# The first three groups of a fused attention and feed-forward kernel: squares moved to ScalarE, factors loaded and multiplied in another way, and another order of calls

## The chip, the cores and the metric

One core of one Trainium2 chip. The time is that of one execution on the device, in microseconds (us), the median of several runs. The engines are named as the profile names them: PE (TensorE), PEld (its weight loads), ACT (ScalarE), DVE (VectorE), POOL (GpSimd) and SP (SyncE, which here only issues DMAs). POOL issues DMAs too, on a queue of its own; that queue takes the loads in which float32 becomes float16.

## The reference

```python
def rmsnorm(x, g):
    rms = np.sqrt(np.mean(x * x, axis=-1, keepdims=True) + 1e-06)
    return x / rms * g
q_n, k_n = rmsnorm(q, g_q), rmsnorm(k, g_k)        # q, k, v: (8, 12, 448, 64)
scores = 1.0 / np.sqrt(64) * np.matmul(q_n, k_n.transpose(0, 1, 3, 2))
scores = scores - np.max(scores, axis=-1, keepdims=True)
attn = np.exp(scores)
attn = attn / (np.sum(attn, axis=-1, keepdims=True) + 1e-09)
attn_out = np.matmul(attn, v)
x = attn_out.transpose(0, 2, 1, 3).reshape(3584, 768)
h = x @ w_in                                       # w_in: (768, 2048)
g = np.maximum(h, 0.0) + alpha * np.minimum(h, 0.0)
out = g @ w_out                                    # w_out: (2048, 768)
```

## The kernel before

There are eight batches of twelve heads. The kernel works in 24 groups `y`, three per batch, each of four heads (two and two, in the two halves of the partitions). A group goes through these steps, each a function that the plan calls:

- `load_qk(y)`: SP loads q and then k of the group, 448 KB each, into buffers. Groups 0, 1, 3 and 4 use four buffers that are lent on in turn; groups 2, 5 and 8 use a part of one large tile, `arena`. A load waits until the last reader of what its buffer held before has finished, and SP issues its loads strictly in order.
- `square(y, q or k)`: x times x; for the first nine groups this is on POOL, with the exception of `square(1,q)`, which is on ACT. `reduce` sums over the 64 elements of a head on DVE, `root` makes x to the power of -0.5 of the mean with two ACT instructions (a logarithm and an exponential), and `scale` multiplies, on DVE for the groups 0 to 3 and on POOL after that. `qs` is the result, in float16.
- `turn(y)`: seven transposes of q and seven of k on PE, and two DVE copies that put them into `qT` and `kT`. The copy of k multiplies by `gain`, the product of g_q and g_k for each of the 64 elements. `turn_one` does it for q or k alone. From group 9 on DVE's own transpose takes its place (`flip`, and `weigh` for the gain).
- `score(y,j)` and `soft(y,j)`, for the seven key tiles j: four matmuls (eight later) into PSUM, then the exponential on ACT.
- `den`, `log`, `invert`: sums over the keys by matmuls with ones, and their reciprocal by a logarithm and an exponential on ACT. `attend` multiplies by v on PE, `times` multiplies by the reciprocal on DVE and writes `xT`. `den(0+1)` and what follows it takes two groups at once, `den(2)` the third one of the batch.

For each batch `b` then follow `up(b,ft)`, for 16 tiles ft of the hidden layer (six matmuls with `w_in_sb`), `slope` (times alpha, mostly on ACT) and `larger` (the maximum, on DVE), which write `gT`; and `down` and `down_end`, the second product and its copy, or from tile 6 on products of sums and differences of blocks (`mix_two`, `qa1` and the like; `mix_weights` prepares them on POOL). For batch 0 `begin(ft)` does four of the six matmuls of the first four tiles before group 2's `xT` is there.

Group 0 is done in pieces by functions of its own: `part_square`, `part_reduce`, `part_root`, `part_scale`, `part_turn`, `part_copy`. `opening()` issues the loads of groups 0 to 2 on SP and those of alpha, g_q and g_k on POOL, and has PE transpose alpha and the g's (tile `ct`), from which `gains()` makes `cols` and `gain` on DVE. `spin(n)` runs matmuls whose result nobody reads.

`load_w_in(c)`, `load_w_out(c)` and `load_v(b)` are issued by POOL. A chunk c of w_in is four loads of 128 KB (as written) for the rows up to 512, and with c even four more for the rest. The completion of POOL's DMAs is counted on eight semaphores in turn, so POOL waits, before it issues a load, until the eighth load before that one has landed.

The order of all this is written out by hand: `PLAN` is a text with 1,325 calls that are made one after the other. Each engine executes its own instructions in the order of the calls; only semaphores stand between engines. A call of the plan moved ahead of another therefore changes the order on each engine that both use, and on no other.

`follow(y, nm)` is a POOL copy of one element that reads `qs`, so that POOL waits at that point for whoever wrote it.

## Time and profile before

| | |
|---|---|
| median of 3 runs | 411.84 us (411.53 to 413.08) |
| the profiled execution | 410.69 us |
| its span, from the first to the last instruction | 408.6 us |
| granted TensorE clock, mean | 1.000 |
| busy: PE, DVE, ACT, POOL | 395.3, 268.3, 270.4, 299.9 us |
| DMA | 58.39 MB moved, 143 GB/s in the mean |

The profile is of one execution. Busy times are shares of the span; a matmul's row includes the time until its result is out, so consecutive rows overlap, and times from row to row are differences of starts. `hT` are the products of `up`, `sc` the scores, `tps` and `tps2` the transposes, `nat` and `arena` the loaded q and k with their squares, `rr` the roots. Queue q1 of the DMA rows is SP's, q0 is POOL's. Lines such as L376 are those of the kernel before.

### The profile page before, as it was taken

To read this page: it belongs to the slowest core of one execution; us is meant where nothing else is said; L and a number is where in the kernel's file an instruction comes from. 1 tells how busy PE (TensorE), PEld (TensorE's weight loads), DVE (VectorE), ACT (ScalarE), POOL (GpSimd) and SP (SyncE) were. 2 spreads that over 40 slices of the span, in tenths; PEclk is the share of its full clock that TensorE was granted. 3 is DMA by queue.
4 is the path that set the end of the run, shared out by engine and by line. 5 is a ranking of instruction groups with operands and counts; after the bars stand their busy time and mean duration, and the time that the engine had idled before them with its cause. 6 is when DMAs were issued, how large, how long until landed. Compare 5 with 4: busy or idle time off the path is not lost.

```text
span 408.6 us, 11992 instructions
## 1 busy us (share of the span) xinstructions
PE 395.3 (97%) x5083; PEld 210.3 (51%) x5083; DVE 268.3 (66%) x480; ACT 270.4 (66%) x405; POOL 299.9 (73%) x200
## 2 busy tenths in 40 slices
PE   7688999999999999999999999999999999999996
PEld 3344445555455445554455455555555455655664
DVE  3957874676766685779678678886668545654422
ACT  5597686757885876767886987686876874245110
POOL 7977998497796998997796995589496809600780
PEclk9999999999999999999999999999999999999999
DMA  7999699796776794579952595794516000230143
GB/s 260 242 280 227 110 265 165 173 239 177 125 180 154 173 203 108 119 172 185 232 130 83 136 240 145 147 217 102 140 38 131 21 2 22 59 79 0 39 98 98
DMA packets 37222, 58.39 MB, mean 143 GB/s; under 512 B 4769, under 2 KB 28977, under 8 KB 37169
## 3 DMA queue, kind: packets, MB, share of 16 engines
q1 hardware_dynamic: 23232, 45.43, 43.2%
q0 software_dynamic: 13536, 11.81, 19.1%
q8 instruction: 39, 0.64, 0.7%
q10 hardware_dynamic: 400, 0.39, 0.3%
q14 instruction: 15, 0.11, 0.1%
HBM read 58.40 MB, written 11.01 MB: 170 GB/s over the span
## 4 chain that ended last, share of the span: by engine, by line
PE 88%; DVE 4%; DMA 3%; POOL 3%; issue 1%; POOLq 0%; DVEq 0%
PE hT L726 25%; PE hTa L726 9%; PE sc L588 8%; PE op L792 7%; PE qx L854 5%; PE av L613 5%; PE qz L854 4%; PE qc L854 4%; PE oq L854 4%; PE qxa L854 3%; PE avb L613 2%; PE dn L613 2%; PE oqm L854 2%; DMA w_in_sb<-in_moe_w_in_dram 2%; POOL nat L376 2%; DMA arena<-in_g_k_dram 2%
## 5 line engine op out<-in xcount | busy, mean ns | idle before, releaser
L602 ACT ACTIVATE expT<-sc 128x896 f16<-128x896 f32 x168 | 146.3, 916 | 40.9 <-PE sc L588 39.2
L726 PE MATMUL hT<-xT,w_in_sb 128*128 128x448 f16 x558 | 115.9, 353 | 1.6 <-DVE xT L709 1.4
L726 PEld LDWEIGHTS <-w_in_sb 128*128 128x128 f16 x768 | 73.0, 98 | 74.5 <-issue 9.9
L423 POOL TENSOR_TENSOR qs<-nat,rr 128x896 f16<-128x896 f32 x30 | 65.7, 2221 | 26.5 <-ACT rr L417 23.4
L766 ACT ACTIVATE gT<-hT,cols 128x448 f16<-128x448 f32 x92 | 58.4, 636 | 40.0 <-PE hT L726 38.9
L772 DVE TENSOR_TENSOR gT<-hT,gT 128x448 f16<-128x448 f32 x93 | 57.3, 619 | 38.2 <-ACT gT L766 37.5
L365 POOL TENSOR_TENSOR nat<-nat 128x896 f32<-128x896 f32 x30 | 50.7, 1697 | 8.1 <-DMA nat<-in_q_dram 7.7
L588 PE MATMUL sc<-qT,kT 64*32 64x448 f16 (+1 forms) x1092 | 49.4, 355 | 4.3 <-ACT expT L602 1.7
L854 PEld LDWEIGHTS <-gT 128*128 128x128 f16 x352 | 33.4, 98 | 25.5 <-issue 4.1
L726 PE MATMUL hTa<-xT,w_in_sb 128*128 128x448 f16 x198 | 42.9, 353 | 0.0
L842 POOL TENSOR_TENSOR gs<-gT 128x1024 f16<-128x1024 f16 x4 | 8.5, 2127 | 36.7 <-DVE gT L772 36.7
L709 DVE TENSOR_TENSOR xT<-av,rden 64x448 f16<-64x448 f32 (+1 forms) x37 | 27.2, 736 | 10.7 <-ACT rden L671 4.6
L386 DVE TENSOR_REDUCE sp<-nat 128x28 f32<-128x896 f32 x30 | 32.1, 1070 | 2.1 <-POOL nat L365 2.0
L588 PEld LDWEIGHTS <-kT 64*32 64x32 f16 (+1 forms) x1092 | 16.7, 93 | 32.4 <-issue 23.0
L792 PE MATMUL op<-w_out_sb,gT 128*128 128x384 f16 x176 | 30.3, 326 | 0.2 <-DVE xT L709 0.2
L766 ACT ACTIVATE gT<-hTa,cols 128x448 f16<-128x448 f32 x33 | 21.0, 636 | 10.5 <-PE hTa L726 10.0
L772 DVE TENSOR_TENSOR gT<-hTa,gT 128x448 f16<-128x448 f32 x33 | 20.4, 618 | 10.6 <-ACT gT L766 10.2
L613 PEld LDWEIGHTS <-vt 64*32 64x32 f16 x1344 | 19.7, 92 | 12.2 <-issue 1.9
L792 PEld LDWEIGHTS <-gT 128*128 128x128 f16 x192 | 18.3, 98 | 14.5 <-issue 3.0
L613 PE MATMUL av<-expT,vt 64*32 64x448 f16 x896 | 24.3, 350 | 0.0
L850 POOL TENSOR_TENSOR gT<-gT 128x1024 f16<-128x1024 f16 x11 | 23.5, 2133 | 0.0
L854 PEld LDWEIGHTS <-arena 128*128 128x128 f16 x136 | 12.6, 98 | 10.5 <-issue 2.3
(151 smaller groups left out, 572.5 us busy)
## 6 DMA issues: line engine op xcount, KB each, us to landing
nat<-in_q_dram SPq DMA_DIRECT2D x60, 216.0 KB, 4.1
nat<-in_k_dram SPq DMA_DIRECT2D x60, 216.0 KB, 5.0
out_dram<-osb SPq DMA_DIRECT2D x107, 96.0 KB, 3.1
vt<-in_v_dram POOLq DMA_DIRECT2D x8, 672.0 KB, 7.8
w_in_sb<-in_moe_w_in_dram POOLq DMA_DIRECT2D x24, 128.0 KB, 7.3
w_out_sb<-in_moe_w_out_dram POOLq DMA_DIRECT2D x4, 768.0 KB, 8.6
nat<-in_k_dram SPq DMA_DIRECT2D x6, 448.0 KB, 7.8
nat<-in_q_dram SPq DMA_DIRECT2D x5, 448.0 KB, 6.7
```

What stands on the lines that cost most here:

```text
L365: nc.gpsimd.tensor_mul(out=sqs[y, nm], in0=t[:, :, :HD], in1=t[:, :, :HD])
L386: nc.vector.tensor_reduce(out=parts[y][:, ts("qk".index(nm), 4 * J), :1], in_=sqs[y, nm], axis=AXIS_X, op=ALU.add,)
L423: nc.gpsimd.tensor_mul(out=t.rearrange("p j d n -> p n j d"), in0=nat[y, nm][:, :, :HD].rearrange("p (n j) d -> p n j d", j=J), in1=r.unsq ...
L588: nc.tensor.matmul(out=sc[ds(64 * g + m * c, m), par, :S].rearrange("p (j c) -> p j c", j=J), lhsT=kT[ds(64 * par, 64), j, g, ts(c, m)], r ...
L602: nc.scalar.activation(out=expT[y][:, j], in_=scs[y, j][:, :, :S], func=AF.Exp, scale=QK_SCALE, bias=EXP_BIAS,)
L613: nc.tensor.matmul(out=accs[g][ds(32 * n, 32), :S], lhsT=weights(g, y, par, c, j), rhs=expT[y][ds(64 * g, 64), j, par, :], start=(j == 0), ...
L709: nc.vector.tensor_mul(out=o, in0=p, in1=q)
L726: nc.tensor.matmul(out=hT[:, :S], lhsT=w_in_sb[:, block_of(g, i), ts(ft, 128)], rhs=xT[b][:, g, i, :], start=(i == 0 and g == 0), stop=(i ...
L766: nc.scalar.activation(out=g, in_=hT[:, :S], func=AF.Copy, scale=alpha_sb[:, ft : ft + 1])
L772: nc.vector.tensor_max(out=g, in0=hT[:, :S], in1=g)
L792: nc.tensor.matmul(out=op[:, :OH], lhsT=gT[:, ft, ts(tile % J, 128)], rhs=w_out_sb[:, ft, ts(oh, OH)], start=(ft == 0), stop=(ft == NF - 1),)
L854: nc.tensor.matmul(out=bank[:, c], lhsT=g[:, ft], rhs=v[:, ft, c], start=(first and ft == 0), stop=(ft == HF - 1), skip_group_check=True,)
```

## The change

Four functions take another form, and the plan is another one up to the scores of group 8, the last of batch 2 (the third batch); from there on it is the same text. In the functions:

- `square` takes the engine and the number of pieces from the plan. Both squares of group 1 are on ACT now, q and k; before, k's was on POOL. `square(2,q)` is one instruction instead of two.
- `opening` loads g_q and g_k with one DMA each, written twice side by side, instead of two, and ahead of alpha. It no longer spins and no longer transposes; `factors()` does that, as a call of the plan, into a score buffer.
- `gains` makes `gain` by a tensor_scalar that reads one factor from PSUM and the other as its scalar.
- `load_w_in(c, lo, hi)` issues a part of the loads of a chunk. `slope` takes its engine from the plan, and `part_copy` could use ACT for k, which the plan doesn't do.

In the plan, the roots of group 0's k are one call, `part_root(k,0:7)`, ahead of group 1's squares, where there were two calls behind `square(1,q)`; k's scales of group 0 stand ahead of `gains()`, and `reduce(1,q)` behind it; the first `spin` calls are others (17 narrow ones first instead of two wide and 17 narrow ones). Further on, `load_qk(3)`, `load_qk(4)` and `load_qk(6)` are called later or earlier than before among calls of other engines, with the same order on SP. w_in's chunk 2 is loaded with its second half first. `times(2,0,0)` stands ahead of `reduce(4,k)`; before, it stood behind it. `soft(2,0)` stands ahead of `soft(1,4)` and `den(0+1,0)`. `scale(7,q)` stands behind `scale(7,k)` and `mix_weights(0,2)`. The calls before and after, up to group 1's first scores:

```diff
-opening() part_square(q,0:1,0:7,act) part_square(q,1:2,0:7,act) part_reduce(q,0:1,0:7) spin(2,0)
-part_reduce(q,1:2,0:7) part_root(q,0:7) part_square(k,0:2,0:3,act) part_scale(q,0:7,7,pool)
-part_reduce(k,0:2,0:3) part_square(k,0:2,3:7,act) square(1,q) load_w_in(1) spin(1)
-part_reduce(k,0:2,3:7) part_root(k,3:7) reduce(1,q) square(1,k) part_root(k,0:3) gains()
-part_turn(q,r0-7) load_qk(3) spin(1,0) part_scale(k,0:3,3,vec) part_turn(k,r0-3)
-part_scale(k,3:7,4,vec) part_copy(q,0:7,vec) part_turn(k,r3-7) load_v(0) reduce(1,k) follow(0,k)
-square(2,q) part_copy(k,0:3,vec) part_copy(k,3:7,vec) root(1) square(2,k) score(0,0,0) soft(0,0)
+opening() part_square(q,0:1,0:7,act) part_square(q,1:2,0:7,act) part_reduce(q,0:1,0:7) spin(17,0)
+part_reduce(q,1:2,0:7) spin(1,0) part_root(q,0:7) part_square(k,0:2,0:3,act)
+part_square(k,0:2,3:7,act) part_scale(q,0:7,7,pool) part_reduce(k,0:2,0:3) part_reduce(k,0:2,3:7)
+spin(2) load_w_in(1,0,4) part_root(k,0:7) part_turn(q,r0-7) part_copy(q,0:7,vec) load_v(0)
+square(1,q,act) spin(3,0) square(1,k,act) factors() spin(3,0) part_scale(k,3:7,4,vec)
+part_scale(k,0:3,3,vec) part_turn(k,r0-3) square(2,q) spin(1,0) square(2,k) gains() reduce(1,q)
+part_turn(k,r3-7) part_copy(k,0:3,vec) part_copy(k,3:7,vec) reduce(1,k) spin(1,0) score(0,0,0)
+score(0,4,1) spin(1,0) load_w_in(0,0,4) soft(0,0) load_w_in(0,4,8) reduce(2,q,1) root(1) spin(1)
```

Around the calls of which the prediction speaks further on:

```diff
-score(2,5,0) square(4,k) load_qk(6) reduce(4,q,None) soft(2,3) soft(2,2) soft(2,5) den(2,0) log(2)
-reduce(4,k,None) invert(2) attend(2,0,1) score(3,0,1) square(5,q) square(5,k) times(2,0,0)
...
-soft(3,2) larger(0,5) up(0,6,0) scale(4,k) turn(4) scale(5,q) up(0,8,0) score(4,0,0) slope(0,6)
+soft(2,5) den(2,0) log(2) square(5,q) invert(2) square(5,k) reduce(4,q,None) attend(2,0,1)
+times(2,0,0) reduce(4,k,None) score(3,1,0) reduce(5,q) square(6,q) reduce(5,k) score(3,0,1) begin(1)
...
+larger(0,2) slope(0,5) larger(0,3) soft(3,2) up(0,6,0) larger(0,5) scale(4,k) load_qk(7) turn(4)
+scale(5,q) up(0,8,0) slope(0,6) soft(3,6) score(4,0,0) square(6,k) scale(5,k) score(3,5,0)
```

The functions:

```diff
-        if (y, nm) == (1, "q"):
-            nc.scalar.activation(out=sqf, in_=src, func=AF.Square)
-        else:
-            n = 2 if (y, nm) in ((2, "q"), (G, "k")) else 1
-            for h in range(n):
-                c = ts(h, 2 * J * D // n)
+        for h in range(n):
+            c = ts(h, 2 * J * D // n)
+            if eng is nc.scalar:
+                nc.scalar.activation(out=sqf[:, c], in_=src[:, c], func=AF.Square)
+            else:
                 nc.gpsimd.tensor_mul(out=sqf[:, c], in0=src[:, c], in1=src[:, c])
...
     def opening():
         load_qk(0)
         nc.scalar.preload_act_table_set("natural_log_exp_and_others")
+        for n, g in enumerate((g_q, g_k)):
+            nc.gpsimd.dma_start(
+                out=rows[NF + n : NF + n + 1].rearrange("o (h d) -> o h d", h=2),
+                in_=g.unsqueeze(0).unsqueeze(0).broadcast_to((1, 2, D)),
+            )
         nc.gpsimd.dma_start(out=rows[:NF], in_=moe_alpha.rearrange("(t p) -> t p", p=128))
-        for n, g in enumerate((g_q, g_k)):
-            for h in range(2):
-                nc.gpsimd.dma_start(
-                    out=rows[NF + n : NF + n + 1, ds(64 * h, 64)], in_=g.unsqueeze(0)
-                )
         load_qk(1, True)
         load_qk(2)
 
-        spin(2)
-        spin(17, False)
-        ct = psf.tile([128, 512], FP32, name="ct", tag="mm")
+    def factors():
+        ct = pss.tile([128, 2, 512], FP32, name="ct", tag="sc")[:, 0]
         nc.tensor.transpose(ct[:, : NF + 2], rows, ident32[: NF + 2, : NF + 2])
         held_ct.append(ct)
 
     def gains():
         nc.vector.tensor_copy(out=cols, in_=held_ct[0][:, : NF + 2])
-        nc.vector.tensor_mul(
-            out=gain, in0=cols[:, NF : NF + 1], in1=cols[:, NF + 1 : NF + 2]
+        nc.vector.tensor_scalar(
+            out=gain, in0=held_ct[0][:, NF : NF + 1], scalar1=cols[:, NF + 1 : NF + 2],
+            scalar2=None, op0=ALU.mult,
         )
```

More of the change, by code (lines that the diff above doesn't have):

```diff
@@ new lines @@
+larger(1,13) larger(1,14) soft(8,3) score(8,5,1) log(6+7) larger(1,15) flip(9,k) weigh(9)
+score(8,1,0) down(3,0,0) scale(10,q) square(11,k) down_end(2,1) score(8,2,0) scale(10,k) flip(9,q)
+soft(8,5) reduce(11,k) reduce(11,q) soft(8,4) soft(8,1) score(8,6,0) fold(11) load_qk(13)
+attend(6+7,0,0) attend(6+7,1,0) score(9,1,0) score(9,0,0) down_end(3,0) soft(8,2) invert(6+7)
+score(9,2,1) down(3,1,0) times(6+7,0,0) soft(8,6) root(11) times(6+7,1,0) load_qk(14) flip(10,q)
+down(4,0,1) mix_weights(1,2) soft(9,0) times(6+7,1,1) score(9,5,0) square(12,q) soft(9,1) soft(9,2)
@@ L358, in load_w_out, with square @@
         )
-    def square(y, nm):
+    def square(y, nm, eng=None, n=1):
         if y >= TD:
@@ L493, in part_copy @@
         tp = tops["ps", nm][:, j]
-        if nm == "k":
+        if nm == "k" and eng is nc.scalar:
+            nc.scalar.activation(out=o, in_=tp, func=AF.Copy, scale=gain[:, 0:1])
+        elif nm == "k":
             nc.vector.tensor_scalar(
```

198 lines of the change are left out of this document (96 added, 102 removed).

## The prediction

> **What bounds the kernel now.** I read the page first, then the busy time by stages, then TensorE's instructions in order of time, and from the places where it stood idle I went back through the other engines' instructions to what they waited for.
>
> ```profile
> span 408.6 us, 11992 instructions
> PE 395.3 (97%) x5083; PEld 210.3 (51%) x5083; DVE 268.3 (66%) x480; ACT 270.4 (66%) x405; POOL 299.9 (73%) x200
> ```
>
> ```profile
> 20.00:30.00 10.00, 8.51 (x157) 4.38 (x160) 5.57 (x9) 9.70 (x15) 7.69 (x12) 1.00 1.12 282
> 30.00:40.00 10.00, 9.57 (x242) 4.85 (x226) 7.19 (x9) 7.75 (x9) 7.31 (x10) 1.00 1.14 240
> 40.00:50.00 10.00, 8.77 (x62) 4.65 (x61) 8.60 (x14) 6.10 (x12) 9.98 (x8) 1.00 0.56 82
> 50.00:60.00 10.00, 9.82 (x80) 4.60 (x78) 7.29 (x11) 8.94 (x13) 9.97 (x8) 1.00 1.16 279
> ```
>
> The columns after the stretch's length are busy us of PE, PEld, DVE, ACT, POOL, then the granted clock, the DMA share and GB/s. Over the span PE is the bound (97%), and from 50 us on it has next to no idle time. What can be won lies ahead of that: the whole of a gain is how much sooner PE comes into its unbroken stretch. ACT is the busy one from 20 to 30 us (9.70), the DMA engines are full (share over 1.1) from 20 to 40 us, and POOL is full from 40 to 60 (9.98, 9.97). So the opening has three limits one after the other, and an edit helps only if it moves the last of them.
>
> ```profile
> 14.24 0.96 PE L588 MATMUL sc<-qT,kT 64*64 64x448 f16 x12 [1.37 <-DVE kT L495]
> 41.30 0.92 PE L726 MATMUL hT<-xT,w_in_sb 128*128 128x448 f16 x4 [1.23 <-DVE xT L709]
> 48.33 0.94 PE L560 MATMUL tps<-ident,qs 128*128 128x128 f16 x14
> 50.59 0.76 PE L588 MATMUL sc<-qT,kT 64*64 64x448 f16 x12 [0.17 <-DVE kT L569]
> ```
>
> These are PE's landmarks: the first score at 14.24, the up product that waited for group 2's attention output until 41.30, and turn(4) at 48.33, seven transposes of q and then seven of k. From 41.30 to 48.33 the timeline shows no idle time.
>
> **The opening, up to the first soft.** In order: start, length, instruction, and in brackets the idle time ahead of it.
>
> ```profile
> 8.32 0.95 ACT L370 ACTIVATE nat<-nat 128x896 f32<-128x896 f32 x1 [0.70 <-DMA nat<-in_q_dram]
> 9.74 0.21 ACT L469 ACTIVATE rr<-rr 128x6 f32<-128x6 f32 x1
> 13.90 0.23 ACT L416 ACTIVATE rr<-ss 128x28 f32<-128x28 f32 x1 [3.94 <-DVE ss L395]
> 14.68 4.97 ACT L602 ACTIVATE expT<-sc 128x896 f16<-128x896 f32 x6 [0.30 <-PE sc L588]
> 7.13 1.21 DVE L457 TENSOR_REDUCE ss<-nat 128x6 f32<-128x384 f32 x2 [2.06 <-ACT nat L450]
> 10.44 0.18 DVE L1029 COPY cols<-ct 128x18 f32<-128x18 f32 x1
> 10.65 0.62 DVE L1030 TENSOR_TENSOR gain<-cols 128x1 f32<-128x1 f32 x1
> 11.19 1.15 DVE L474 TENSOR_TENSOR qs<-nat,rr 128x384 f16<-128x384 f32 x2
> 12.26 0.61 DVE L501 COPY qT<-tps 128x896 f16<-128x896 f16 x1
> 12.79 1.07 DVE L395 TENSOR_REDUCE ss<-nat 128x14 f32<-128x896 f32 x1
> 13.79 0.79 DVE L495 TENSOR_SCALAR kT<-tps,gain 128x384 f16<-128x384 f16 x2
> ```
>
> k's sums are ready at 7.13+1.21 = 8.34, but ACT stands behind square(1,q), which waits for its load until 8.32, so k's roots end only at 9.74+0.21 = 9.95. In the changed kernel one pair of roots for k comes before that square: two instructions of 0.21, ending near 8.8. DVE then does the copy of qT (0.61) from 8.34 and k's two scales (1.07 without overlap) from 8.95 to 10.0, where before it began them at 11.19. The factors' matmul stands in PE's queue ahead of k's transposes; it waits for the loads of g and alpha.
>
> ```profile
> 3.82 6.24 DMA arena<-in_g_k_dram
> ```
>
> The last g load lands at 10.06. Two loads are gone and alpha goes last, so I take 9.5 to 10.1 for all three. The waiting transposes then run near 10.4 to 11.1 (the three filling matmuls behind the factors included), beside DVE's cols and gain (0.2 and about 0.5 until the next could start: 10.65 to 11.19) and reduce(1,q) (1.0). The kT copies (0.6) end at 12.5 to 12.8, the first soft starts at 13.0 to 13.3, and before it was 14.68: **1.4 to 1.7 us earlier on ACT**. The tensor_scalar in place of the product for gain is one DVE instruction for another; I cost it at nothing, and if it took 0.3 us longer that would come off this lead only. The second group's k squares on ACT cost about 0.95 (row L370), in a stretch in which ACT had 3.94 us idle.
>
> **Softs, up to the up products.** From 14.68 ACT is nearly continuous, so a lead at the first soft carries on while squares and roots keep up. I do not expect all of it: soft(2,0) now stands before soft(1,4), so the denominators, and with them log(0+1), come one soft (4.97 for six, so 0.83) later in ACT's order, and score(1,0) now follows reduce(2,k) and the qT copy on DVE. I take a lead of 0.9 at invert(2).
>
> ```profile
> 37.69 0.95 ACT L671 ACTIVATE rden<-rden 128x896 f32<-128x896 f32 x1
> 39.16 1.09 DVE L395 TENSOR_REDUCE ss<-nat 128x14 f32<-128x896 f32 x1 [0.55 <-POOL nat L376]
> 40.16 1.08 DVE L709 TENSOR_TENSOR xT<-av,rden 128x896 f16<-128x896 f32 x1
> ```
>
> Before, invert(2) ended at 38.6, but times(2,0,0) stood on DVE behind reduce(4,k), which waited for POOL's square: it ran at 40.16. Now it stands behind reduce(4,q) alone. With POOL as before, square(4,q) ends at 37.47 (35.80+1.67, rows below), reduce(4,q) at about 38.55, times at about 39.6. PE's up products would restart at 39.7 instead of 41.30: **1.6 us earlier**, and at turn(4) PE would arrive at 48.33-1.6 = 46.7.
>
> **Where the gain stops: POOL at turn(4).**
>
> ```profile
> 9.52 1.72 POOL L376 TENSOR_TENSOR nat<-nat 128x896 f32<-128x896 f32 x1
> 32.59 0.56 POOL L339 DMA_DIRECT2D w_in_sb<-in_moe_w_in_dram  x1 [1.10 <-DMA w_in_sb<-in_moe_w_in_dram]
> 34.08 1.71 POOL L339 DMA_DIRECT2D w_in_sb<-in_moe_w_in_dram  x3 [0.93 <-DMA w_in_sb<-in_moe_w_in_dram]
> 35.80 3.33 POOL L376 TENSOR_TENSOR nat<-nat 128x896 f32<-128x896 f32 x2
> 39.08 3.31 POOL L376 TENSOR_TENSOR arena<-arena 128x896 f32<-128x896 f32 x2
> 42.36 1.67 POOL L376 TENSOR_TENSOR nat<-nat 128x896 f32<-128x896 f32 x1
> 43.98 0.95 POOL L353 DMA_DIRECT2D w_out_sb<-in_moe_w_out_dram  x1
> 44.95 1.70 POOL L436 TENSOR_TENSOR qs<-nat,rr 128x896 f16<-128x896 f32 x1
> 46.73 1.68 POOL L436 TENSOR_TENSOR qs<-nat,rr 128x896 f16<-128x896 f32 x1
> ```
>
> The last row is scale(4,k): it ends at 48.4. PE began k's half of turn(4) half a row after 48.33, at about 48.7 to 48.8. So in the kernel before POOL was only about 0.35 us ahead of PE there, with not one idle us on POOL between 34.08 and 48.4. The changed kernel has the same five squares, the same w_out load and the same two scales in that order behind its last w_in(3) load, and the same PE work ahead of turn(4). PE's 1.6 us are therefore spent waiting at turn(4), unless POOL gets out of its w_in(3) loads sooner.
>
> POOL does shed work ahead of that: square(1,k) (1.72, first row) goes to ACT. But POOL isn't short of time there, it waits for landings (1.10 and 0.93 in the rows): the first load of w_in(3) may go out only when the first load of w_in(2) has landed, the next when the second has, and so on, in both kernels. What POOL saves earlier becomes a longer wait if those landings stay.
>
> ```profile
> q0 software_dynamic: 228, 0.20, 62.1%
> q1 hardware_dynamic: 198, 0.35, 53.8%
> ...
> q1 hardware_dynamic: 416, 0.70, 99.0%
> ```
>
> ```profile
> DMA to landing us min/median/max: 5.3/7.3/10.1
> ```
>
> The first two rows are the queues from 16 to 18 us, the third SP's queue alone from 6 to 8; then POOL's 24 weight pieces from issue to landing. When both queues have work they share 16 full engines, and the stages from 20 to 40 us (1.12 and 1.14 above) leave nothing idle. Ahead of the second piece of w_in(2) the changed kernel has to move the same bytes: the same q and k loads of groups 0 to 5, the same v, the same w_in pieces. Issuing some of them 1 to 2 us sooner can't make full engines deliver them sooner. I take a shift of POOL's release of -0.2 to +0.2, at the middle nothing.
>
> The Trainium skill would have it otherwise: "DMA: Bandwidth & Descriptors", section "Anatomy of one DMA — SWDGE (gpsimd) path", gives such a load about 2.0 us plus its bytes at 436 GB/s, an estimate of 2.3 us for 128 KB; by that none of POOL's waits would exist. The row's 5.3 to 10.1 speaks against it under this load.
>
> **Behind turn(4)** PE has no wait of over 0.2 us for others until 60 us (50.59 above), and the order of PE's work is nearly the same. One place is tighter than before: scale(7,q) now stands behind scale(7,k), a weight mix and one more soft, and I find POOL about 0.2 us ahead of PE at turn(7); 0 to 0.4 us could go there.
>
> **The sum.** Gain at turn(4): 0.35 (POOL's lead) plus the shift of -0.2 to +0.2, less 0 to 0.2 at turn(7): about 0.3. The profiled execution took 410.69 us, 2.1 more than its span, and the median of the runs is 411.84, so 1.15 above it. I predict **411.5** by the median, or 410.4 for a profiled execution. A measurement can tell 0.5%, 2.06 us here, from no change.
>
> **Rivals.**
> - *POOL's pieces land as much sooner as they are issued.* w_in(2)'s first piece goes out about 1.1 us sooner (1.72 less for the square, less a longer wait for v). For it: the release is what it waits for, not the engines' total. Against: shares over 1. Then POOL is 1.1 earlier, PE gains 1.4: 410.4.
> - *POOL doesn't wait at all*, because pieces come quickly when k's and q's loads are no longer in the way. POOL's idle of 1.10+0.93 and the square's 1.72 are over 3 us, and the bound is then ACT: times(2,0,0) right after invert(2) at 37.7 puts the up products at 38.8, 2.5 sooner: 409.3. This is also what the skill's fixed cost would give.
> - *Slower: SP's loads overtake the w_in pieces.* k's scale for group 0 ends 2.2 us sooner, scale(1) and scale(2) 0.5 to 2, and each frees a buffer for which a load waits on SP.
>
> ```profile
> nat<-in_k_dram SPq DMA_DIRECT2D x6, 448.0 KB, 7.8
> 31.05 0.37 SPq L306 DMA_DIRECT2D nat<-in_q_dram  x1
> ```
>
> A load of 448 KB at 0.70 MB in 2 us is 1.3 us of all engines. Before, group 6's q went out at 31.05 and so mostly missed the pieces for which POOL waits (until 33.8). If it gets ahead of them, POOL is released 1.3 later, PE waits at turn(4) for 49.7 and 0.35 is lost to 1.3: 0.95 slower, 412.8; with k of group 6 too, 2.25 slower, 414.1. It decides from a shift of 0.35 on. Against it: scale(3,q) is only about 0.4 us sooner by the working above. The skill's page "DMA: Bandwidth & Descriptors", section "Queues, rings and completion order", says that each engine takes turns between its queues packet by packet; by that an earlier SP load takes half of the engines' time from POOL's pieces from the moment it arrives, which is this rival's mechanism, and the shares of 62.1% and 53.8% agree.
> - *The earlier first soft doesn't come about* (the g loads land late and the factors hold PE's queue). Up to about 1.3 us at turn(4) is spare, so the time would be the same 411.5.
>
> **Chances.** The forecast, the last rival with it, 0.60; pieces sooner 0.14; no waits 0.12; SP's loads ahead 0.14, half of that with both loads. Faster by over 0.5% (below 409.8) needs the third case and a tail of the second: 0.15. Slower by over 0.5% (above 413.9) needs the fourth with both loads, and I leave something for a stall that I haven't seen: 0.10. The rest, 0.75, is no change. The range reaches from the third case to the fourth with one load: 409.3 to 412.9.
>
> **What would show it.** Right: the first soft near 13.2, the up products near 39.7, POOL's w_in(3) loads with longer waits than 1.10 and 0.93 that end near 35.8, scale(4,k) ending near 48.4, and a new idle of about 1.3 us on PE ahead of k's half of turn(4). Wrong, if that idle is missing: then POOL's loads landed sooner and the gain is 1.4 or more; or if scale(4,k) ends after 49, then slower.

## The result and the profile after

| | before | after |
|---|---|---|
| median, 18 executions each | 411.92 us (410.60 to 415.94) | 414.41 us (412.14 to 423.90) |
| ratio of after to before | | 1.0054, 95% interval 1.0031 to 1.0077 |
| the profiled execution | 410.69 us | 415.97 us |
| its span | 408.6 us | 414.1 us |
| granted TensorE clock, mean | 1.000 | 0.991 |

The change costs half a per cent; 411.5 had been forecast, with 409.3 to 412.9. Ratios here and below leave out executions over 1.5% above the fastest of their kernel; of the changed kernel these are 4 of 18, at 420.0 to 423.9, and the experiments below make a cause in the kernel likely, so they are counted where it is at stake.

The page of the changed kernel, the lines of the span and of the busy times:

```profile
span 414.1 us, 12003 instructions
PE 399.4 (96%) x5092; PEld 210.9 (51%) x5092; DVE 269.9 (65%) x480; ACT 270.7 (65%) x404; POOL 299.1 (72%) x197
```

The instructions of its opening, in order of time for one engine after the other (ACT, DVE, POOL, PE); line numbers are 2 higher than before:

```profile
9.16 0.21 ACT L469 ACTIVATE rr<-rr 128x14 f32<-128x14 f32 x1
15.50 0.92 ACT L604 ACTIVATE expT<-sc 128x896 f16<-128x896 f32 x1 [4.44 <-PE sc L590]
9.95 0.62 DVE L503 COPY qT<-tps 128x896 f16<-128x896 f16 x1 [1.07 <-PE tps L485]
10.49 2.65 DVE L474 TENSOR_TENSOR qs<-nat,rr 128x512 f16<-128x512 f32 x2
13.27 0.22 DVE L1031 TENSOR_SCALAR gain<-ct,cols 128x1 f32<-128x1 f32 x1
11.05 1.67 POOL L376 TENSOR_TENSOR arena<-arena 128x896 f32<-128x896 f32 x1 [0.48 <-DMA arena<-in_q_dram]
13.20 0.34 PE L485 MATMUL tps<-ident,qs 128*128 128x128 f16 x3 [1.89 <-DVE qs L474]
```

k's roots end at 9.37, sooner than before (9.95) but later than foreseen (near 8.8), as k's load landed at 7.10 and not at 6.55. DVE's copy of qT, which stands ahead of k's scales, waits until 9.95 for q's transposes: their input is there at 7.52, but TensorE runs filling matmuls ahead of them until 9.36. So k's two scales begin at 10.49 and not at 8.95. And they, which took 1.15 us before, take 2.65, and in that time POOL runs a product of its own, square(2,q), from 11.05 to 12.72. TensorE stands idle for 1.89 us ahead of k's transposes, and the first soft starts at 15.50: not 1.4 to 1.7 us earlier than before, but 0.8 later. The busy times by stages show what follows on TensorE (after the six pairs of busy times: the granted clock, the DMA share, GB/s):

```profile
12.00:14.00 2.00, 0.80 (x9) 0.55 (x9) 1.97 (x4) 0.00 (x0) 1.55 (x2) 1.00 1.19 217
14.00:16.00 2.00, 1.29 (x10) 0.50 (x10) 2.00 (x4) 0.50 (x1) 2.00 (x4) 0.52 1.25 205
16.00:18.00 2.00, 2.00 (x7) 0.55 (x6) 2.00 (x4) 1.56 (x4) 2.00 (x4) 0.50 1.21 256
18.00:20.00 2.00, 2.00 (x18) 0.63 (x14) 1.24 (x2) 0.92 (x1) 0.62 (x2) 0.50 1.19 253
```

The clock is halved from 14 to past 20 us. Further on, the instructions around the up products and turn(4) (DVE, POOL, PE):

```profile
36.50 1.50 DVE L436 TENSOR_TENSOR arena<-nat,rr 128x896 f16<-128x896 f32 x1
43.41 1.09 DVE L711 TENSOR_TENSOR xT<-av,rden 128x896 f16<-128x896 f32 x1 [2.29 <-ACT rden L673]
32.65 2.47 POOL L344 DMA_DIRECT2D w_in_sb<-in_moe_w_in_dram  x4 [0.24 <-DMA w_in_sb<-in_moe_w_in_dram]
35.14 4.40 POOL L376 TENSOR_TENSOR nat<-nat 128x896 f32<-128x896 f32 x2
47.86 1.68 POOL L436 TENSOR_TENSOR qs<-nat,rr 128x896 f16<-128x896 f32 x1
39.84 1.51 PE L615 MATMUL dn<-expT,ones 64*32 64x448 f16 x55 [0.41 <-issue]
43.11 2.44 PE L728 MATMUL hT<-xT,w_in_sb 128*128 128x448 f16 x12
52.07 0.94 PE L562 MATMUL tps<-ident,qs 128*128 128x128 f16 x14
```

The first eight of the twelve products at 43.11 are the ones that need no wait; the first that did wait before, at 41.30, runs here at 44.63, since its data are there only at 44.50 (the row of 43.41), and turn(4) at 52.07 (48.33): 3.7 us of the 5.5 by which the span is longer have gone by then. There is no idle time ahead of k's half of turn(4). Nearly all of the rest goes at one place at 94 us:

```profile
92.37 0.23 ACT L416 ACTIVATE rr<-ss 128x28 f32<-128x28 f32 x1 [2.75 <-DVE ss L395]
91.20 1.07 DVE L395 TENSOR_REDUCE ss<-arena 128x14 f32<-128x896 f32 x1
82.60 1.69 POOL L436 TENSOR_TENSOR qs<-nat,rr 128x896 f16<-128x896 f32 x1 [8.03 <-ACT rr L417]
94.89 0.57 PE L590 MATMUL sc<-qT,kT 64*64 64x448 f16 x8 [1.54 <-DVE gT L774]
```

This score needs the bank of up(1,1), which larger(1,1) frees; larger(1,1) needs slope(1,1), which stands on ACT behind root(8), and root(8) waits until 92.3 for reduce(8,q) (the DVE row), which the new order puts behind reduce(9,q). No such wait was there before.

### The profile page after: what moved, and what is told of

It reads as the page before. It is cut to its first block, busy times and chain, and to the rows that moved or that the text cites. A ratio compares the mean times of both kernels' runs of the same rounds, so it can differ in the third digit from the quotient of the medians.

```text
span 414.1 us, 12003 instructions
## 1 busy us (share of the span) xinstructions
PE 399.4 (96%) x5092; PEld 210.9 (51%) x5092; DVE 269.9 (65%) x480; ACT 270.7 (65%) x404; POOL 299.1 (72%) x197
## 4 chain that ended last, share of the span: by engine, by line
PE 88%; ACT 4%; DVE 4%; DMA 1%; issue 1%; POOL 0%; ACTq 0%; POOLq 0%; DVEq 0%
PE hT L728 25%; PE hTa L728 9%; PE sc L590 9%; PE op L794 5%; PE qx L856 5%; PE av L615 5%; PE qz L856 4%; PE qc L856 4%; PE oq L856 3%; PE dn L615 3%; ACT expT L604 3%; PE avb L615 3%; PE spin L1002 3%; PE qxa L856 3%; PE oqm L856 2%; PE qza L856 1%
```

## The experiments

One execution has several causes in it, so the parts were taken one by one. All ratios are to the kernel before, timed on the same chip.

**Where in the order?** a_head has the changed functions and calls up to turn(4) and the old order from there; a_rest the old calls up to turn(4) and the changed order from there; fn_only the changed functions under the old order throughout.

> The changed kernel's calls up to and with turn(4), then the remaining calls in the order of the kernel before (the changed kernel's functions). Opening theory (the loss comes from the first 50 us: k's scales on DVE beside POOL's square, then a halved PE clock): turn(4) as late as in the changed kernel, 51 to 52.5 in the profile, and a time 1.0 to 4 us above the kernel before. Later theory (the loss is the stall of 1.5 us that PE has at 93 us, behind root(8)): no stall of over 0.5 us behind turn(4), and a time within 1 us of the kernel before. Both at work: 1.5 us less than the changed kernel, so some 413.

> The other half: the calls of the kernel before up to and with turn(4), then the remaining calls in the changed kernel's order. Opening theory: turn(4) at 48.3 as before and a time within 0.5 us of the kernel before. Later theory: the stall of about 1.5 us ahead of group 6's scores is there, and the time is 1.2 to 2 us above the kernel before.

> The changed functions (factors by two loads, the tensor_scalar for the gain, the pieces of w_in's loads, squares with an engine to choose) with the order of calls before, the first group's second square again on GpSimd. If the loss is the order's alone: the time as before, 411.5 within 0.4. If two loads in place of four, or the gain by tensor_scalar, cost something themselves: 412 and more. Theory A says that the stream has as many instructions as before on TensorE, so no late block: restart of the up products near 41.3.

| kernel | median us | ratio | interval |
|---|---|---|---|
| a_head | 413.32 | 1.0015 | 0.9985 to 1.0044 |
| a_rest | 413.97 | 1.0059 | 1.0033 to 1.0085 |
| fn_only | 412.26 | 0.9990 | 0.9964 to 1.0015 |

The functions (two loads, the tensor_scalar, the pieces) cost nothing that can be told; the order does. The order from turn(4) on costs by itself as much as the whole change, and a_rest's trace has the same wait of 1.54 us at a score. Not all of its loss need be that wait: its turn(4) came at 49.44 and not at the expected 48.3, with the old calls up to there. The head brings no gain and shows no loss of its own, though it should have gained; 4 of its 12 executions took 420.9 to 423.2.

**The wait at 94 us.** a_reduce8 is the changed kernel with one edit:

```diff
-turn(7) ... reduce(9,q) ... reduce(8,q) ... root(8)
+turn(7) ... reduce(8,q) root(8) reduce(9,q)
```

> The changed kernel with reduce(8,q) and root(8) moved ahead of reduce(9,q), as they stand in the kernel before. Later theory: the stall of 1.54 us at 93 us goes, and the time falls by 1.2 to 1.6 us against the changed kernel. Opening theory alone: no change within 0.5 us.

412.64 us, ratio 1.0025 (1.0006 to 1.0044): some 0.3% are gone, though the interval still overlaps that of the change (1.0031 to 1.0077); 2 of its 12 executions took 420.7 and 421.7 us. TensorE's row at that place:

```profile
90.51 0.57 PE L590 MATMUL sc<-qT,kT 64*64 64x448 f16 x8 [0.55 <-DVE gT L774]
```

One us of the 1.54 is gone and the ratio falls by 0.3%, or 1.2 us: about what a wait costs that is paid in full, as it would be here, where TensorE has no other idle time around it.

**Why does the head gain nothing?** In a_head nothing disturbed the opening: the first score started at 12.87, and it was ahead until the up products. Its instructions there (PE, then DVE):

```profile
38.74 1.69 PE L728 MATMUL hT<-xT,w_in_sb 128*128 128x448 f16 x8
42.31 0.92 PE L728 MATMUL hT<-xT,w_in_sb 128*128 128x448 f16 x4 [1.88 <-DVE ss L395]
39.04 1.09 DVE L711 TENSOR_TENSOR xT<-av,rden 128x896 f16<-128x896 f32 x1 [1.42 <-ACT rden L673]
```

The data for the products (the DVE row) are there at 40.13; TensorE starts at 42.31. The releaser named, a sum of squares on DVE, feeds nothing there. What stands just ahead of 42.31 on TensorE are waits for four weight loads, which had landed by 31.7; the first of these waits is recorded at 42.09. So the instruction itself was late. The counts of instructions that had begun before the wait (the pairs x after PE and PEld), by the stages view from 0 to just ahead of the restart, of a_head, a_follow (below) and a_reduce8:

```profile
0.00:42.00 42.00, 33.19 (x478) 15.43 (x478) 27.87 (x42) 29.83 (x46) 32.49 (x49) 1.00 1.04 246
```

```profile
0.00:42.70 42.70, 33.71 (x478) 15.84 (x478) 28.06 (x43) 29.82 (x46) 33.13 (x50) 1.00 1.04 242
```

```profile
0.00:41.40 41.40, 33.70 (x478) 15.64 (x478) 26.63 (x41) 29.38 (x44) 32.18 (x48) 1.00 1.04 249
```

With five records of other kinds (bare waits above all) that makes 961 instructions ahead of the wait each time. Other waits without a releaser, in the changed kernel at 39.84 ("issue") and in a_rest at 76.68, come behind 705 and 1729 instructions: 256 fewer, and three times 256 more. And the DMA view of a_head from 39.5 to 40.7 us shows one packet of instructions among those of the loads:

```profile
q0 software_dynamic: 125, 0.11, 56.1%
q1 hardware_dynamic: 112, 0.18, 46.2%
q8 instruction: 1, 0.02, 5.8%
```

Queue q8 carries instructions, 16 KB each, 39 or 40 packets in a run of some 10,200 TensorE records: one for every 256. The packet ends at 40.67, and TensorE goes on at 42.09. In a_follow the ends are 41.21 and 42.78, in a_reduce8 39.91 and 41.41: 1.4 to 1.6 us later each time. In the kernel before, the packet ends at 40.47, but the weight load of the waiting product is number 948, ahead of the block's end, and TensorE crosses that end only at 42.43. At the counts of 705 and 1729 the step from a packet's end to the instruction that came late is much the same: from 38.49 to 39.84 in the changed kernel, from 75.25 to 76.68 in a_rest. So the theory: TensorE's code for the up products comes in a block that arrives near 40 us behind full DMA engines, and the earlier restart runs into it. Three kernels were made to test it. b_fetch is the kernel before with 14 more instructions and the same TensorE time; a_lean is the changed kernel with follow(0,k) and 36 fewer; h_lean is a_head with these two edits.

```diff
b_fetch:
-score(0,3,0) spin(1) ... score(1,3,0) spin(1)
+score(0,3,0) spin(5,0) ... score(1,3,0) spin(6,0)
a_lean, h_lean:
-spin(17,0) ... spin(3,0) ... spin(3,0) ... spin(2,0) ... spin(2,0)
+spin(3) ... spin(1,0) ... spin(1)
-square(2,q)
+follow(0,k) square(2,q)
```

> The kernel before, with two of its wide filler matmul pairs of the opening (1.0 us each at full clock) replaced by 5 and 6 narrow ones (0.19 us each): the same time on TensorE, 14 more instructions in its stream. Theory A: TensorE's instructions come in blocks of 256 over the DMA engines, and the fourth block ends at the record numbered 961 in every trace. In the kernel before, the first up product that waits stands at number 948, in front of that end, so the late block is hidden; with 14 more it stands at 962, and TensorE has to wait for the block: its packet ends near 40.5 us and TensorE went on 1.4 to 1.6 us after that in three traces, so the up products restart near 42.0 instead of 41.3 and the whole gets 0.4 to 0.8 us longer, about 412.2. Theory B: the wait that the trace puts down to VectorE's sums is real, and the number of instructions doesn't matter: restart at 41.3, the time as before within 0.2 us.

> The changed kernel with the mark copy ahead of the third group's squares (as a_follow) and 36 instructions fewer on TensorE in the opening: 17 narrow fillers as 3 wide ones, three narrow ones as one, three as one wide one, and two pairs left out. Theory A (the block of code comes late): the end of the fourth block moves 36 instructions on, some 3 us of up products behind the restart, so nothing waits for it; the restart goes from 43.0 (a_follow) to about 40.6, when the weighted sums of the second pair are done, TensorE reaches turn(4) at 47.7 and POOL's factors for it end near 47.5: turn(4) comes 2.3 us earlier than in a_follow, and the time is 1.5 to 2.3 us below a_follow, 411.5 to 412.2, with the stall of 1.5 us near 93 still there. Theory B: no gain, 413.7, or a loss where the filler that was left out lets the clock drop.

> The changed kernel's order up to turn(4), then the order before (as a_head), with the mark copy ahead of the third group's squares and the same 36 instructions fewer on TensorE. Theory A: the restart moves from 42.3 to about 40.2 and turn(4) from 49.35 to 47.4, where POOL's factors bind; no stall near 93. 409.9 us of span less 1.9: a time near 410, 1 to 1.5 us below the kernel before. Theory B: as a_head, 411.8 to 413.3.

| kernel | median us | ratio | interval |
|---|---|---|---|
| b_fetch | 412.85 | 1.0018 | 0.9993 to 1.0043 |
| a_lean | 412.30 | 0.9998 | 0.9975 to 1.0021 |
| h_lean | 411.18 | 0.9962 | 0.9935 to 0.9988 |

TensorE in b_fetch:

```profile
42.39 0.93 PE L726 MATMUL hT<-xT,w_in_sb 128*128 128x448 f16 x4 [1.55 <-DVE ss L395]
```

The kernel before now waits as well, in the record that was foreseen, until 42.38, 1.6 us after its packet's end at 40.78; its span is 1.1 us longer, and its median 0.8 higher, although the interval of the ratio still includes 1. A restart near 42.4 alone would prove little: fn_only and a_rest, with the old calls up to there, restart at 42.41 and 42.40, because their data are there only at 42.36 and 42.35. In b_fetch the data were there at 40.92. In the two with fewer instructions the wait for code is gone. TensorE, and at the end POOL's scale(4,k), in h_lean:

```profile
38.84 2.54 PE L728 MATMUL hT<-xT,w_in_sb 128*128 128x448 f16 x12
44.89 1.29 PE L728 MATMUL hT<-xT,w_in_sb 128*128 128x448 f16 x6 [1.24 <-DVE gT L774]
48.90 0.94 PE L562 MATMUL tps<-ident,qs 128*128 128x128 f16 x14
47.51 1.68 POOL L436 TENSOR_TENSOR qs<-nat,rr 128x896 f16<-128x896 f32 x1
```

The up products run through. 1.24 us come back at 44.89, because larger(0,0) stands on DVE behind reduce(5,k), which waits for POOL's squares until 43.2. And scale(4,k) ends at 49.19, 0.1 us before k's half of turn(4) starts, with no idle time ahead of it: POOL is just in time there, and what it costs TensorE is the 1.24 us. From a_head to h_lean, with two edits, the ratio falls from 1.0015 to 0.9962; from a_follow to a_lean, from 1.0041 to 0.9998.

The number of instructions isn't the only difference between these pairs, since fewer fillers also let the opening go sooner: the first score starts at 11.98 in a_lean and 13.39 in a_follow. But the data for the up products are only 0.45 us sooner in a_lean (40.19 against 40.64), and the products restart 2.76 sooner (40.24 against 43.00). In h_lean the data are even later than in a_head (40.41 against 40.13), and the products restart 1.84 sooner (40.47 against 42.31). What isn't shown is where h_lean gains on the kernel before: it was expected near 410, and its traced execution, of 411.07 us, reaches turn(4) at 48.90, where the kernel before, in an execution of 410.69, has it at 48.33.

**The long scales, and the long executions.** a_follow is the changed kernel with the mark copy of the old order (a copy on POOL that waits for a scale of k; in the changed order this is the first of the two) ahead of square(2,q). a_share goes the other way: a_follow with square(1,q) on POOL, so that a POOL product always runs beside k's scales; a_share_spin is a_share with seven more fillers on TensorE in that time.

```diff
a_follow:
-square(2,q)
+follow(0,k) square(2,q)
a_share, from a_follow:
-square(1,q,act)
+square(1,q)
a_share_spin, from a_share:
-factors() spin(3,0)
+factors() spin(10,0)
```

> The changed kernel with one call more, follow(0,k) ahead of square(2,q): POOL's square waits until k's last scale on DVE is done. Theory that POOL's square and DVE's scale hold each other up: the two scales take 1.15 us instead of 2.65, the first soft is at 14.0 instead of 15.5, PE is idle for 0.5 us instead of 1.9 ahead of k's transposes, so that its clock is less often halved; the time falls by 1 to 2.5 us against the changed kernel. Rival, that the scale is long by itself in this place (its data or the roots come late): it stays at 2.65 and the time does not change. Second rival, that POOL then releases w_in later and takes the gain back: first soft 14.0, turn(4) not sooner.

> a_follow with the first group's second q square (square(1,q)) on GpSimd in place of ScalarE: GpSimd then runs a product of 128x896 from 10.6 to 12.3, beside VectorE's two scales of k, in every execution. If the two engines slow each other (in the changed kernel's profile the scales took 2.65 us beside GpSimd's squares, 1.15 in the kernel before): the scales take 2.0 to 2.7 us, the first score starts 1.0 to 1.5 us after a_follow's 13.39, and the granted clock drops for some us behind that in most executions. The whole: by 0.3 to 1.0 us more than a_follow where the late code block hides part of it, 1 to 3 more where the clock drops. If the 2.65 us had another cause (the data late): the scales stay at 1.15 and the time as a_follow, 413.7.

> a_share with seven more narrow fillers on TensorE ahead of k's transposes, which keep it busy through the longer scales. If it is TensorE's idle time there that brings the clock down: the scales are as long as in a_share, the clock stays at 1.00 from 14 to 20 us, and the 12 scores of the first step start at the same time but take 0.96 us and not 1.3; the spread of the runs gets smaller. If the clock drops for another reason: the granted clock is 0.5 there as well. The 14 more instructions move the end of the code block ahead of the restart by some 0.6 us of work, which changes nothing that the late block doesn't set already.

a_follow: 413.70 us, ratio 1.0041 (1.0016 to 1.0065), none of 12 above 415.5, its scales not lengthened, the first score at 13.39 and the first soft at 13.83. So the scale was long because of POOL's square; but the time is only 0.1% below the change, where 1 to 2.5 us had been expected, and its up products stood until 43.00 for their code all the same. a_share: 425.41, with 3 of 4 executions at 425.2 to 426.4 and one at 414.7. a_share_spin: all four at 421.7 to 426.8, ratio 1.0310 (1.0271 to 1.0349). That is far more than was expected, and the instructions of a_share show how (DVE, POOL, then PE):

```profile
10.49 6.03 DVE L474 TENSOR_TENSOR qs<-nat,rr 128x512 f16<-128x512 f32 x2
38.33 6.81 DVE L436 TENSOR_TENSOR arena<-nat,rr 128x896 f16<-128x896 f32 x1 [3.14 <-ACT rr L417]
10.56 2.14 POOL L376 TENSOR_TENSOR nat<-nat 128x896 f32<-128x896 f32 x1
12.79 3.31 POOL L376 TENSOR_TENSOR arena<-arena 128x896 f32<-128x896 f32 x2
37.60 3.33 POOL L376 TENSOR_TENSOR nat<-nat 128x896 f32<-128x896 f32 x2
40.88 3.31 POOL L376 TENSOR_TENSOR arena<-arena 128x896 f32<-128x896 f32 x2
45.73 0.91 PE L562 MATMUL tps<-ident,arena 128*128 128x128 f16 x7 [4.54 <-DVE xT L711]
```

Here a DVE product of two operands in SBUF that met a row of POOL products ended just after the row: 16.52 after POOL's 16.10, and, for scale(3,q), 45.14 after POOL's 44.19. Alone, the second of k's scales takes 0.55 and scale(3,q) 1.09. TensorE waits 5.26 us ahead of k's transposes for the first, and 4.54 (the last row) behind the second; in a_share_spin it is scale(3,k) that takes 8.83. The Trainium skill, "SBUF — State Buffer", section "Who interferes with whom", says that a DVE instruction with two inputs in SBUF contends with a POOL instruction that reads SBUF, and that the pair of ports which the two share is an exclusive lock: whoever issues first has it for the whole instruction and the other blocks fully. The trace agrees that the one blocks, but here DVE didn't get its turn after one instruction: it stood through three POOL products the first time and four the second. It isn't always so. In the changed kernel's trace (the row of 36.50) scale(3,k) met the same row of POOL's squares and had its turn behind the first of them; it took 1.50, and POOL's second square, which now met it, 2.52 in place of 1.68. What decides who comes next is open. The tensor_reduces (1.07), and products with one operand in PSUM (1.08 to 1.09 for the times of 128x896), aren't lengthened beside POOL in these traces.

The clock, in the same stages, of a_share and then of a_share_spin:

```profile
14.00:16.00 2.00, 0.00 (x0) 0.00 (x0) 2.00 (x1) 0.00 (x0) 2.00 (x2) 0.52 1.25 203
16.00:18.00 2.00, 1.42 (x9) 0.93 (x9) 1.90 (x5) 0.00 (x0) 2.00 (x5) 0.50 1.24 196
```

```profile
14.00:16.00 2.00, 1.28 (x12) 0.57 (x11) 2.00 (x4) 0.62 (x1) 2.00 (x2) 1.00 1.26 207
16.00:18.00 2.00, 1.88 (x13) 0.41 (x12) 2.00 (x4) 1.96 (x5) 2.00 (x4) 1.00 1.19 250
```

With TensorE filled, the clock stays; but in a_share_spin's profile the scales took 2.73 and not 6.03 us as well, so fillers and a shorter wait can't be told apart in these two. The changed kernel's own trace is the nearer comparison: there the scales took 2.65, TensorE with three fillers stood idle for 1.89 us, and the clock was halved; here, with ten, it stood for 0.64, and the clock stayed at 1.00. That the idle time halves the clock is likely; with one trace of each, and a square on another engine between them, it is not settled.

**Is it the lock that makes executions of 420 us?** A second place for it is scale(3,q) and scale(3,k) on DVE beside the fifth group's squares on POOL. In the old order POOL stands at its w_in(3) loads just then, which keeps it away. h_best is h_lean with these loads behind scale(4,k). h_two adds to it a mark copy that waits for scale(3,k); a_mend is a_lean with a_reduce8's edit, and a_mend2 adds the same mark copy to that.

```diff
h_best, from h_lean:
-load_w_in(3,0,4) ... scale(4,k)
+scale(4,k) load_w_in(3,0,4)
h_two, a_mend2, from h_best, a_mend:
-square(4,q) ... scale(3,k)
+scale(3,k) follow(3,k) square(4,q)
```

> h_lean with the last four w_in loads on GpSimd's queue moved from ahead of the fifth group's squares to behind scale(4,k). In h_lean GpSimd stood 1.05 us and more at these loads, began the squares at 36.6 and ended scale(4,k) at 49.16, where the second half of turn(4) starts at once; VectorE's sum of squares behind square(5,k) at 43.2 holds larger(0,0) and TensorE 1.24 us at 44.9. Theory A (with the code block out of the way GpSimd's queue is the bound, as the prediction had it): the squares begin near 33.5, scale(4,k) ends near 46.2, the wait of 1.24 us goes, TensorE reaches turn(4) at 47.6 and finds it ready: 1.0 to 1.3 us less than h_lean, 410.0 by the medians, 0.993 to 0.994 of before. Theory B: TensorE's own stream or SP's late transfers bind and the time stays at h_lean's 411.2.

> a_lean with reduce(8,q) and root(8) ahead of reduce(9,q), as in a_reduce8: the changed order with its three faults mended (mark copy, code block, stall near 93). If the three add up: 0.9 us below a_lean, 411.4, 0.997 to 0.998 of before, with 0.5 left of the stall near 93. If the stall near 93 is only filled by another wait: as a_lean, 412.3.

> h_best with one instruction more: a mark copy on GpSimd (follow(3,k)) ahead of the fifth group's squares, which waits until VectorE has scaled the fourth group. In h_best's profile VectorE's scale of that group took 6.89 us beside GpSimd's row of products (1.09 alone) and 9 of 12 executions took 418 to 420 us, the other three 410.3 to 412.7. Theory A (a VectorE product with two operands in SBUF gets no turn while GpSimd's products follow on one another): the scale takes 1.09 in every execution, none is near 418, the squares begin near 34.4, scale(4,k) ends near 47.1, TensorE reaches turn(4) at 47.7: 1.0 us less than h_lean, a median of 410.2, 0.993 to 0.995 of before. Theory B (the long executions come from the transfers that meet when the loads of w_in go out later): executions near 419 stay, as in h_best.

> a_mend with the same mark copy ahead of the fifth group's squares. a_mend had 9 executions at 410.3 to 412.2 and 3 at 421 to 423. Theory A: none above 415, the others as a_mend or up to 0.4 later, as GpSimd's squares wait for scale(3,k): a median of 411.4 to 411.8, 0.997 to 0.999 of before. Theory B: as a_mend, with a quarter of the executions at 421 to 423.

| kernel | executions | above 418 us | median us | ratio | interval |
|---|---|---|---|---|---|
| h_best | 12 | 9 | 419.41 | 0.9973 | 0.9939 to 1.0007 |
| h_two | 12 | 0 | 411.81 | 0.9995 | 0.9968 to 1.0022 |
| a_mend | 12 | 3 | 411.64 | 0.9977 | 0.9952 to 1.0002 |
| a_mend2 | 12 | 0 | 411.29 | 0.9972 | 0.9943 to 1.0000 |

One of h_best's nine had a mean TensorE clock of 0.65 and took 588.6 us; that clock is something else, and what lowered it isn't known. This is also the only execution of h_best that was traced. In it scale(3,q) stood beside four of POOL's squares, which end at 39.16:

```profile
33.22 6.89 DVE L436 TENSOR_TENSOR arena<-nat,rr 128x896 f16<-128x896 f32 x1 [3.57 <-ACT rr L417]
```

The other eight lie at 418.2 to 420.3, and the mark copy alone takes all of them away. DVE's scale(3,q) and scale(3,k), and POOL's mark copy and squares, in h_two:

```profile
29.42 1.09 DVE L436 TENSOR_TENSOR arena<-nat,rr 128x896 f16<-128x896 f32 x1 [0.55 <-ACT rr L417]
32.48 1.09 DVE L436 TENSOR_TENSOR arena<-nat,rr 128x896 f16<-128x896 f32 x1 [0.91 <-POOL mark L509]
33.64 0.19 POOL L509 COPY mark<-arena 128x1 f16<-128x1 f16 x1 [1.19 <-DVE arena L436]
33.78 3.31 POOL L376 TENSOR_TENSOR nat<-nat 128x896 f32<-128x896 f32 x2
```

Both scales take 1.09. That the later loads make the executions long (theory B) is ruled out, since h_two has these loads where h_best has them. For a_mend, and for the changed kernel's executions at 420 to 424, the collision is the likely cause and not a traced one: of h_best's, a_mend's and the changed kernel's long executions, only the one of 588.6 us has a trace. POOL is far earlier (scale(4,k) ends at 46.4), and TensorE is 1.5 us ahead of the kernel before in the scores behind turn(4) (49.07 against 50.59), but the median isn't: expected was 410.2. In the profiled execution 0.46 us go at 69.5 and 0.73 at 75.6, the latter again a block of code that is late (number 1729); where the rest of the lead goes is open.

a_mend's edits add up: 0.2% less than a_lean, though the intervals overlap. The first twelve up products follow one another without a gap there, the ninth, which waits for the data, at 37.89 + 8 x 0.19 = 39.4:

```profile
37.89 2.44 PE L728 MATMUL hT<-xT,w_in_sb 128*128 128x448 f16 x12
```

**A version that beats both.** h_mend is h_lean with the second mark copy and the w_in(3) loads where they were.

> h_lean with the mark copy ahead of the fifth group's squares, the w_in loads where h_lean has them: the changed opening with 36 fewer instructions on TensorE and both mark copies, then the order before. If the mark copies keep VectorE's and GpSimd's products apart at no cost: none of the executions above 415 (h_lean had one at 421 in 12), the others as h_lean's 409.4 to 412.4, 0.995 to 0.998 of before. If the mark copy holds GpSimd where h_lean's waits for the w_in loads didn't: up to 0.5 us more, no difference from before.

410.98 us (409.66 to 413.20, 12 executions, none above 415), ratio 0.9968 (0.9947 to 0.9990). By the medians it is 0.3% faster than the kernel before, with an interval that ends just below 1, and by the two ratios 0.9% faster than the change. Where it gains on the kernel before isn't shown: in its traced execution, of 411.74 us, the data for the up products came at 41.91 (41.24 before) and turn(4) at 49.48 (48.33).

## Why the prediction was wrong, step by step

What the median lost goes back to two steps. The up products were to restart as soon as their data are there, and TensorE's code came later (42.09 against 40.13 in a_head). And behind turn(4) 0 to 0.4 us was put down where a wait of 1.54 came about. The other terms in order:

- **The opening.** The gain (0.22 in place of 0.62) and the squares on ACT (1.77 for both) cost no more than worked out. Two steps failed. The first is the start of k's scales, 8.95 in the forecast and 10.49 in the run: k's load and with it the roots (9.37) came later, and the step had DVE's copy of qT at 8.34 without asking when TensorE would run q's transposes, which stood behind fillers; the copy ran at 9.95. In a_lean, with fewer fillers, it ran at 8.58. The matmul of the factors ran at 10.41, about when expected but for another reason: its loads had landed by 8.93, not 9.5 to 10.1, and fillers and q's transposes held it. The second is "k's two scales (1.07 without overlap)". It was taken from a row in which POOL happened to be kept off by the mark copy follow(0,k), which the change drops; square(2,q) beside them made 2.65 of it. The step didn't ask what the removed mark copy had held apart. With the copy back, the first soft starts at 13.83 (a_follow). In a_head, without a collision, it starts at 13.31, at the edge of the 13.0 to 13.3 forecast; since its scales began at 10.01, that is partly luck.
- **The clock** wasn't in the sum at all. In the profiled execution it was halved for more than six us after TensorE's wait for those scales.
- **Up products at 39.7.** The chain of data was right where nothing disturbed the opening: a_head had them ready at 40.13, and a_mend started them at 39.4. (In the changed kernel's own trace, behind the long scales and the halved clock, they came only at 44.50.) What failed is that data alone set the restart. The block of TensorE's code let it go on at 42.09 in a_head; the kernel before needed that block only at 42.43. The changed order gives TensorE 16 more instructions ahead of the waiting product (its weight load is number 964 in place of 948), and the block's end comes in between.
- **The cap by POOL at turn(4)** didn't come about in the changed kernel: no idle time ahead of k's half, since TensorE itself came late. Nor did POOL's w_in(3) waits grow: 0.24 us in place of 1.10 and 0.93, with an end at 35.1. POOL was released 0.7 us sooner, where at most 0.2 had been allowed for. The argument took the same bytes to be ahead of POOL's pieces; here SP's loads went out later than before (group 5's q at 25.35 in place of 22.27), and whether that is why isn't shown. In a_lean and h_lean these loads end at 36.4 and 36.6, later than before, so the term was too narrow both ways. In h_lean, where TensorE was ahead, scale(4,k) ended 0.1 us before k's half of turn(4), so the cap was near; but TensorE had waited for POOL before that, at larger(0,0).
- **Behind turn(4)** "0 to 0.4 us could go" at turn(7). The place and the way were near (roots and sums in a changed order on ACT and DVE), but it was reduce(8,q) and root(8) and a score that pays: 1.54 us, and with one us of it removed the ratio is 0.3% lower. This term was mis-sized by a factor of four, since only turn(7) was followed through its queues.
- **The rival on the slower side** (SP's loads overtaking w_in's pieces) isn't what happened: q of group 6 went out later than before (35.58 against 31.05). None of the rivals was a collision of two engines in SBUF or late code.

How the loss is made up, by ratios whose intervals overlap: a_reduce8 puts 0.3% on the wait at 94 us; a_follow against a_lean puts 0.4% on the late block and the sooner opening together; the first collision, and the clock behind it, lie in the 0.1% between the changed kernel and a_follow and, with the second collision, probably in the 4 of 18 executions at 420 to 424, which the ratio doesn't count. With all three mended, a_mend's median of 411.64 is close to the 411.5 that was forecast for the change. The traced execution of the changed kernel is not the typical one: at 415.97 it is 1.6 above the median. In it TensorE's waits for code come to the 0.41 at 39.84, as its data were late as well.

## What to carry to other kernels

A small instruction whose only effect is a wait (a mark copy) may be what keeps two engines out of each other's way: before dropping it, list what can then overlap, and look for products of two SBUF operands on VectorE beside GpSimd's. A wait whose named releaser feeds nothing there is a wait for something else; count the engine's instructions up to it, and if the number recurs, it is code that is late, which filler instructions bring on and fewer of them remove. In a part where the bounding engine has no idle time, every root or sum that moves in a queue has to be followed to the last one who waits.

## What the runs showed of the hardware

- TensorE's instructions arrive in packets of 16 KB, one per 256, and TensorE went on 1.4 to 1.6 us after the packet's end in four traces (a_head, a_follow, a_reduce8, b_fetch). With the DMA engines full, packets of 1.0 to 1.3 us came too late for the up products near 40 us. The Trainium skill, "Runtime: NRT & Kernel Launch", section "Instruction fetch mechanics", has the block of 256 instructions and calls the crossing mostly hidden; here a crossing cost up to 2.05 us (a_follow, where the data had been there since 40.64).
- A DVE product with both operands in SBUF took 5.4 and 6.8 us beside three and four POOL products in a row (a_share), and 0.55 and 1.09 alone; in the changed kernel one had its turn behind the first POOL product, and took 1.50. Where DVE was first (k's second scale in a_follow and h_lean, beside POOL for 0.4 us), its product took the usual 0.55.
